# Signs of float64 weights by a ScalarE activation, softmax inverses on GpSimd, and weight scales from whole norms, with a new order

## The chip, the cores and the metric

One core of a Trainium2 chip runs the kernel. A core has a matrix engine (TensorE, PE in the profile; its weight loads are PEld), a vector engine (VectorE, DVE), an activation engine (ScalarE, ACT), GpSimd (POOL) and SyncE (SP), which here only issues DMAs. Each engine works through its own queue in the order in which the program put the instructions there. The metric is the device time of one execution in microseconds (us).

## The reference

Three blocks follow one another: attention with a banded or a strided causal mask, a dense layer with a softmax-weighted activation and a layer norm, and a bilinear layer. All inputs come as float32 here but the weights, which come as float64.

```
def _attn_ref(q, k, v):                       # 4 batches, 8 heads, 576 positions, 64 wide
    scores = scale * np.matmul(q, k.transpose(0, 1, 3, 2))
    ...                                       # heads 0-3: last 32 positions; 4-7: every 32nd
    attn = np.exp(scores - np.max(scores, axis=-1, keepdims=True))
    attn = attn / (np.sum(attn, axis=-1, keepdims=True) + 1e-09)
    return np.matmul(attn, v)

def _moe_ref(x, w_in, w_out, g_ln):           # 2304 tokens, 512 -> 1024 -> 512
    h = x @ w_in
    e = np.exp(h - h_max)
    solu = h * (e / (np.sum(e, axis=-1, keepdims=True) + 1e-09))
    ln = (solu - mu) / np.sqrt(var + 1e-06) * g_ln
    return ln @ w_out

def _moe2_ref(x, w_a, w_b, w_out):            # 512 -> 1536 -> 512
    return (x @ w_a) * (x @ w_b) @ w_out
```

## The kernel before

The kernel collects its work as a list of operations, each with an engine, an estimated duration, the tokens that it reads and writes, and a key. A planner (class `Plan`) orders them: `forward` lists the operations by a model of the engines, taking the ready one with the smallest key; `backward` lists them from the end and gives new keys; `schedule` repeats this `passes` times with some random noise on the keys and keeps the order with the smallest modelled length. The program is then emitted in that order, so every engine's queue is a result of the planner.

The work has these parts:

- *Attention* (`att_tile`): 40 tiles, ten for each of four batches: four strided ones with 6 cells of 54 columns, and six banded ones with 4 or 2 cells of 96. Scores on PE (L700, L703), row maxima on DVE (L716), differences on DVE (L725), exponentials on ScalarE (L728), row sums on DVE (L729), then the inverse of the sums: ScalarE adds a small number and scales (L733), DVE takes the reciprocal (L734). GpSimd multiplies (L767 in batch 0, which goes to PE for its transposes, L763; L778 in the others, which are split into two float16 parts by L785 and L786 and transposed by DMA). The product with V is L797 in batch 0 and L802 to L804 in the others.
- *Weights from float64* (`from_f64`): a DMA brings 128x512 numbers as pairs of 32-bit words into one of three buffers `raw64`. ScalarE scales the upper words, read as float32, by 2^-112 (L462), which moves the exponent; DVE shifts the lower words (L464), merges both (L469), and sets the sign from the upper word (L475), the last reader of the buffer. There are 52 such conversions: 8 for `w_in`, 8 for the first layer's `w_out`, 36 for the bilinear layer's three matrices (12 of them during attention, `early`).
- *First layer* (`moe1`, `s2`): 18 token tiles. The first product h (L855) needs `w_in` in two parts; softmax and layer norm follow (L860 to L884), a DMA transposes, and the second product y (L904) needs all eight pieces of the first layer's `w_out`, split into two float16 parts by ScalarE (L540) and DVE (L542) after a scale that depends on all of them.
- *Bilinear layer* (`product`, `ab`, `out_tile`): products M (L1288) and output products o (L1353), by three passes over parts of the weights. For the scale of a pair of weight tiles the kernel squares both (`norms_ab`, L915, to bfloat16), lets PE sum the squares of each column over the partitions with a matrix of ones (L920, eight matmuls for a pair, collected in the bank `y` or `Q`), and takes the largest (`scale_ab`, from L927).

PSUM bank `y` has one buffer. It is shared by y, the transposes of batch 0 and the norms of the early weights.

## Time and profile before

| what | value |
|---|---|
| median of 3 runs | 745.37 us (742.57 to 747.46) |
| profiled execution | 743.58 us |
| its span | 741.8 us, 14239 instructions |
| PE busy | 713.4 us (96%) |
| DVE busy | 522.9 us (70%) |
| ScalarE busy | 430.1 us (58%) |
| GpSimd busy | 121.8 us (16%) |
| mean granted clock of PE | 0.986 of full speed |

The span runs from the first to the last instruction of the profiled execution; its own time is 1.8 us longer. The page gives, for groups of equal instructions, busy time and mean duration, and beside these the idle time ahead of them with what ended it. DVE and ScalarE instructions overlap their neighbours in the records by some hundredth parts of a microsecond, so sums of durations lie above busy times. Matmuls are pipelined; what one of them costs PE is read from the distance to the next start.

### The profile page before, as it was taken

How to read it: one execution, taken by the hardware profiler on the slowest of the kernel's cores; microseconds unless marked ns; L12 is line 12 of the kernel's file. 1: busy time of each engine (PE TensorE's matmuls, PEld its weight loads, DVE VectorE, ACT ScalarE, POOL GpSimd, SP SyncE). 2: the span in 40 equal slices, each digit the busy share in tenths (PEclk: the TensorE clock that was granted, in tenths of full speed). 3: DMA queues.
4: the chain of work that ended last, by engine and by line, in shares of the span. 5: the costliest groups of instructions: out<-in, count | busy, mean ns of one | idle time of the engine just before them, and what ended most of it. 6: DMA issues, size and time to landing. Idle time of an engine off the chain costs nothing.

```text
span 741.8 us, 14239 instructions
## 1 busy us (share of the span) xinstructions
PE 713.4 (96%) x5516; PEld 474.5 (64%) x5516; DVE 522.9 (70%) x1020; ACT 430.1 (58%) x800; POOL 121.8 (16%) x194
## 2 busy tenths in 40 slices
PE   6889899999999999989999999999999999999997
PEld 4667678878778887867655555555555545555553
DVE  5899989666758676898998998758576454434252
ACT  4678887677678667885767656555272323132230
POOL 5441425243425332120000000000000000000000
PEclk9979899999999999999999999999999999999999
DMA  9889969978683944967547133507505041611304
GB/s 213 198 213 207 212 167 183 228 172 179 123 146 84 232 87 115 272 129 250 198 152 263 33 122 100 163 29 236 197 29 170 1 130 47 230 57 55 117 5 166
DMA packets 159328, 109.62 MB, mean 148 GB/s; under 512 B 103702, under 2 KB 137500, under 8 KB 159260
## 3 DMA queue, kind: packets, MB, share of 16 engines
q1 hardware_dynamic: 159260, 108.71, 56.5%
q8 instruction: 43, 0.70, 0.4%
q14 instruction: 25, 0.20, 0.1%
HBM read 65.42 MB, written 27.53 MB: 125 GB/s over the span
## 4 chain that ended last, share of the span: by engine, by line
PE 89%; DVE 4%; ACT 3%; issue 2%; DMA 1%; POOL 0%; DVEq 0%; ACTq 0%; SPq 0%
PE M L1288 33%; PE o L1353 19%; PE h L855 13%; PE y L904 12%; PE s L703 4%; PE s L618 2%; PE xbank L802 2%; PE xbank L797 1%; ACT qkT L626 1%; PE s L700 1%; DVE wk L863 1%; PE xbank L804 1%; PE xbank L803 1%; DMA raw<-in_moe_w_out_dram 1%; DVE e L725 1%
## 5 line engine op out<-in xcount | busy, mean ns | idle before, releaser
L1288 PE MATMUL M<-y,w 128*128 128x384 f16 x1512 | 256.0, 326 | 0.0
L1288 PEld LDWEIGHTS <-w 128*128 128x128 f16 x1512 | 147.3, 98 | 100.0
L1353 PE MATMUL o<-wo,p 128*128 128x512 f16 x648 | 147.0, 379 | 0.0
L1353 PEld LDWEIGHTS <-p 128*128 128x128 f16 x648 | 63.3, 98 | 71.7
L904 PE MATMUL y<-lnT,wout 128*128 128x256 f16 x864 | 101.1, 273 | 2.4 <-DMA lnT<-ln 1.0
L904 PEld LDWEIGHTS <-wout 128*128 128x128 f16 x864 | 82.1, 98 | 15.4 <-issue 4.8
L855 PE MATMUL h<-win,xh 128*128 128x512 f32 x288 | 79.7, 416 | 4.6 <-DVE wk L863 2.5
L1295 ACT COPY M<-M 128x384 f32<-128x384 f32 x72 | 33.6, 467 | 58.5 <-PE M L1288 58.2
L855 PEld LDWEIGHTS h<-win,xh 128*128 128x128 f32 x288 | 54.2, 196 | 16.3 <-ACT xh L844 3.1
L1360 DVE SCALAR_TENSOR_TENSOR ob<-o,osc,op 128x512 f32<-128x512 f32 x36 | 27.0, 751 | 46.3 <-PE o L1353 41.8
L1338 ACT ACTIVATE p<-A 128x384 f16<-128x384 f32 x72 | 37.2, 522 | 36.0 <-DVE A L1337 35.7
L1299 DVE TENSOR_TENSOR A<-M,V 128x384 f32<-128x384 f32 x36 | 19.9, 555 | 34.7 <-PE M L1288 34.5
L1340 DVE SCALAR_TENSOR_TENSOR p<-A,p 128x384 f16<-128x384 f32 x72 | 39.0, 553 | 7.4 <-ACT p L1338 6.4
L1310 ACT COPY V<-M 128x384 f32<-128x384 f32 x36 | 17.1, 474 | 42.4 <-PE M L1288 42.2
L855 PE MATMUL h<-win,xl 128*128 128x512 f32 x144 | 41.3, 411 | 0.0
L703 PE MATMUL s<-qkT 64*54 64x54 f32 (+2 forms) x672 | 37.2, 247 | 3.3 <-ACT qkT L626 2.3
L462 ACT ACTIVATE f64f<-raw 128x512 f32<-128x512 f32 x52 | 34.8, 672 | 9.1 <-DVE w L1127 4.9
L469 DVE SCALAR_TENSOR_TENSOR f64f<-f64f,raw 128x512 int32<-128x512 int32 x52 | 37.1, 717 | 1.0 <-ACT f64f L462 0.3
L703 PEld LDWEIGHTS s<-qkT 64*54 64x54 f32 (+2 forms) x672 | 26.9, 138 | 14.0 <-issue 3.9
L786 POOL TENSOR_TENSOR P<-e,P 128x324 f16<-128x324 f32 (+2 forms) x30 | 30.7, 1029 | 19.9 <-ACT P L785 19.9
L1337 DVE TENSOR_TENSOR A<-A,M 128x384 f32<-128x384 f32 x36 | 19.9, 553 | 19.5 <-PE M L1288 19.4
L855 PEld LDWEIGHTS h<-win,xl 128*128 128x128 f32 x144 | 28.0, 199 | 6.1
(168 smaller groups left out, 1127.0 us busy)
## 6 DMA issues: line engine op xcount, KB each, us to landing
raw<-in_moe_w_out_dram SPq DMA_DIRECT2D x20, 512.0 KB
o_scr<-ob SPq DMA_DIRECT2D x36, 256.0 KB
op<-o_scr SPq DMA_DIRECT2D x36, 256.0 KB
raw<-in_moe_w_a_dram SPq DMA_DIRECT2D x12, 512.0 KB
raw<-in_moe_w_b_dram SPq DMA_DIRECT2D x12, 512.0 KB
y_scr<-y SPq DMA_DIRECT2D x14, 384.0 KB
y<-y_scr SPq DMA_DIRECT2D x14, 384.0 KB
y_scr<-ys SPq DMA_DIRECT2D x18, 256.0 KB
```

The lines of the kernel that those rows point to most:

```text
L462: act(0.67, lambda: nc.scalar.activation(f(), raw()[:, :, 1].bitcast(F32), AF.Copy, scale=2.0 ** -112), (raw,), (f,))
L469: nc.vector.scalar_tensor_tensor(fi, fi, 3, raw()[:, :, 0], op0=ALU.logical_shift_left, op1=ALU.bitwise_or)
L703: nc.tensor.matmul(s[64 * half:64 * half + nq, f, col:col + kk], g.T()[w, 0, q0:q0 + nq], g.T()[w, 1, k0:k0 + kk], start=False, stop=n == ...
L786: pool(0.15 + 1.4 * pl, lambda: nc.gpsimd.tensor_tensor(plo, ev(), ph, op=ALU.subtract), (e, ("P2", pi, 0)), (("P2", pi, 1),))
L855: nc.tensor.matmul(h()[:, 512 * n:512 * n + 512], xs[xa]()[:, kk], win[wa][:, kk, 512 * n:512 * n + 512], start=(pi == 0 and kk == 0), sto ...
L904: nc.tensor.matmul(y()[:, 256 * mi:256 * mi + 256], wout[:, kk, wa, 128 * m:128 * m + 128], lnT()[:, xa, kk], start=(pi == 0 and kk == 0), ...
L1288: nc.tensor.matmul(bank()[:, :HB], w()[:, wa, a, kk], y7[b]()[:, xa, kk], start=first and pi == 0 and kk == 0, stop=pi == 2 and kk == 1, s ...
L1295: act(TA, lambda: nc.scalar.copy(dst()[:, :HB], src()[:, :HB]), (src,), (dst,))
L1338: act(TA, lambda x=x, v=v: nc.scalar.activation(v(0), x(), AF.Copy, scale=2.0 ** -PEXP), (x,), ((pu, 0, c, t),))
L1340: dve(TD, lambda x=x, v=v: nc.vector.scalar_tensor_tensor(v(1), x(), 2.0 ** -PEXP, v(0), op0=ALU.mult, op1=ALU.subtract), (x, (pu, 0, c, t ...
L1353: nc.tensor.matmul(o(), pus[u]()[:, xa, c, 128 * tt:128 * tt + 128], wo()[:, 2 * u + c, wa], start=(u == 0 and c == 0 and pi == 0), stop=( ...
L1360: dve(0.75, lambda: nc.vector.scalar_tensor_tensor(ob(), o(), osc()[:, tt:tt + 1], op(), op0=ALU.mult, op1=ALU.add), (o, osc, op), (ob,))
```

## The change

- *Signs.* In `from_f64` ScalarE's `Copy` becomes `Prelu` with the same scale and a slope of 2^32 for negative values. A negative number then carries 2^32 more in its exponent field, and the merge's shift by three bits turns that into the sign bit. DVE's sign instruction goes; the merge (now L475) writes the destination and is the buffer's last reader.
- *Inverses.* In `att_tile` the ScalarE addition and DVE's reciprocal become two GpSimd instructions: an addition and a product with constants, and a power with exponent -1 from a small tile of -1.
- *Norms.* `norms_ab` lets ScalarE sum the squares along a row as it squares; `scale_ab` sums these over the partitions with one float32 matmul of two columns (ones 128x128 as weights) and takes the larger of two numbers. The scale is from the norm of a whole half tile, not of its largest column. The PSUM bank is taken only for that product.
- *Planner.* 120 passes instead of 40, a third of the noise, and from the 40th pass on a return to the best keys every 12 passes. Options that weren't in use are removed.

```diff
-PARAM = dict(early=(0,), seed=1, noise=0.3, ... passes=40, e=3,
+PARAM = dict(back=12, first=40, early=(0,), seed=1, noise=0.1, ... passes=120, e=3,
@@ schedule
         for n in range(PARAM["passes"]):
+            if n % PARAM["back"] == 0 and n >= PARAM["first"]:
+                for o, key in zip(self.ops, keys):
+                    o.key = key
+                self.shift = shift
+                self.forward()
             self.backward()
@@ constants
+        nc.gpsimd.memset(mone, -1.0)
@@ from_f64
-            act(0.67, lambda: nc.scalar.activation(f(), raw()[:, :, 1].bitcast(F32), AF.Copy, scale=2.0 ** -112),
-                (raw,), (f,))
+        act(0.67, lambda: nc.scalar.activation(f(), raw()[:, :, 1].bitcast(F32), AF.Prelu, scale=2.0 ** -112,
+                                               alpha=2.0 ** 32), (raw,), (f,))
         dve(0.5, lambda: nc.vector.tensor_scalar(raw()[:, :, 0], raw()[:, :, 0], 29, None,
                                                   op0=ALU.logical_shift_right), (), (raw,))
-        def sign():
-            nc.vector.scalar_tensor_tensor(g().bitcast(I32), raw()[:, :, 1], -2 ** 31, f().bitcast(I32),
-                                           op0=ALU.bitwise_and, op1=ALU.bitwise_or)
-        dve(0.76, merge, (raw,), (f,))
...
-            dve(0.75, sign, (raw, f, *need), w)
+        def merge():
+            nc.vector.scalar_tensor_tensor(g().bitcast(I32), f().bitcast(I32), 3, raw()[:, :, 0],
+                                           op0=ALU.logical_shift_left, op1=ALU.bitwise_or)
+        dve(0.76, merge, (raw, f, *need) if dtok else (raw, *need), w)
@@ att_tile
-        act(0.2, lambda: nc.scalar.activation(s4()[:, :ng], s4()[:, :ng], AF.Copy, scale=u, bias=1e-9 * u), (), ss)
-        dve(0.17, lambda: nc.vector.reciprocal(r()[:, :ng], s4()[:, :ng]), ss, (r,))
+        def inverse():
+            nc.gpsimd.tensor_scalar(s4()[:, :ng], s4()[:, :ng], 1e-9, u, op0=ALU.add, op1=ALU.mult)
+            nc.gpsimd.tensor_tensor(r()[:, :ng], s4()[:, :ng], mone[:, :ng], op=ALU.pow)
+        pool(0.75, inverse, ("small",), (*ss, r))
@@ norms_ab, scale_ab
-        act(0.61, lambda: nc.scalar.activation(sq(), f(), AF.Square), (f,), (sq,))
-            for c in range(4):
-                nc.tensor.matmul(tp()[:, w], onesb, sq()[:, 128 * c:128 * c + 128], start=c == 0, stop=c == 3)
-        pe(4 * 0.06, norms, (sq, "small"), ((tp, i),), 512)
+        act(0.82, lambda: nc.scalar.activation(sq(), f(), AF.Square, accum_out=fro[:, u, m, i:i + 1]), (f,),
+            (sq, ("fro", u, m, i)))
+        pe(0.12, lambda: nc.tensor.matmul(tp()[:, :2], ones_sq, fro[:, u, m], start=True, stop=True),
+           [("fro", u, m, i) for i in range(2)] + ["small"], (tp,), 8)
-            nc.vector.tensor_reduce(x, tp()[:, :256], axis=AX.X, op=ALU.max)
+            nc.vector.tensor_reduce(x, tp()[:, :2], axis=AX.X, op=ALU.max)
```

The planner moves instructions on every engine. Three places follow, each as the program of before and of the change puts it into one queue.

On DVE, the second and third conversion of the first layer's `w_out`, before: shift (L464), merge (L469) and sign (L475), with reciprocals of attention sums (`sm` to `r`) between them.

```order
L464 TENSOR_SCALAR raw_637<-raw_637 128x512
L469 SCALAR_TENSOR_TENSOR f64f<-f64f,raw_637 128x512
L475 SCALAR_TENSOR_TENSOR wout<-raw_637,f64f 128x512
L464 TENSOR_SCALAR raw_678<-raw_678 128x512
L734 RECIPROCAL r<-sm_702 128x2
L469 SCALAR_TENSOR_TENSOR f64f<-f64f,raw_678 128x512
L734 RECIPROCAL r<-sm_727 128x2
L475 SCALAR_TENSOR_TENSOR wout<-raw_678,f64f 128x512
```

The same place on DVE now, where L469 is the shift, L475 the merge, L723 a row sum, and L857 the first row maximum of h:

```order
L469 TENSOR_SCALAR raw_639<-raw_639 128x512
L723 TENSOR_REDUCE sm_727<-e 128x2
L475 SCALAR_TENSOR_TENSOR wout<-f64f,raw_639 128x512
L469 TENSOR_SCALAR raw_669<-raw_669 128x512
L475 SCALAR_TENSOR_TENSOR wout<-f64f,raw_669 128x512
L469 TENSOR_SCALAR raw_702<-raw_702 128x512
L475 SCALAR_TENSOR_TENSOR wout<-f64f,raw_702 128x512
L857 TENSOR_REDUCE st<-h 128x1
```

Three instructions became two and the reciprocals are gone, so eight rows hold three conversions where they held two. Four conversions of `w_out` stand ahead of h's first row maximum in both programs. Up to the last split of `w_out` (L542, row 172 of DVE's queue before; L536, row 132 now) there were 17 signs, 18 shifts, 18 merges and 15 reciprocals; now there are 16 shifts and 16 merges, and the other groups differ by one small reduction each.

On GpSimd, the first products of batch 0, before (L767 the product with the inverse, L491 a split of `w_in`):

```order
L767 TENSOR_TENSOR lnT<-e,r 128x6x54
L491 TENSOR_TENSOR win_108<-f64f,win_107 128x512
L767 TENSOR_TENSOR lnT<-e,r 128x6x54
L491 TENSOR_TENSOR win_108<-f64f,win_107 128x512
L767 TENSOR_TENSOR lnT<-e,r 128x6x54 x2
```

The same place on GpSimd now, where L729 adds and scales, L730 is the power, L764 the product and L485 the split:

```order
L729 TENSOR_SCALAR sm_257<-sm_257 128x6
L730 TENSOR_TENSOR r<-sm_257,small 128x6
L764 TENSOR_TENSOR lnT<-e,r 128x6x54
L729 TENSOR_SCALAR sm_287<-sm_287 128x6
L730 TENSOR_TENSOR r<-sm_287,small 128x6
L764 TENSOR_TENSOR lnT<-e,r 128x6x54
L485 TENSOR_TENSOR win_108<-f64f,win_107 128x512
```

Two instructions stand ahead of each product, and the first split of `w_in` comes behind two products instead of one.

On SP, the first loads before (L568 and L574 are q and k, L585 is v, L457 a float64 load):

```order
L568 DMA rawq<-in_q_dram 96x6x128
L568 DMA rawk<-in_k_dram 96x6x128
L568 DMA rawq<-in_q_dram 96x6x128
L568 DMA rawk<-in_k_dram 96x6x128
L457 DMA raw_177<-in_moe_w_in_dram 128x1024
L585 DMA raws_110<-in_v_dram 18x5x128
```

And now (L562 and L568 are q and k, L579 is v, L465 a float64 load):

```order
L562 DMA rawk<-in_k_dram 96x6x128
L579 DMA raws_110<-in_v_dram 18x6x128 x2
L568 DMA rawq<-in_q_dram 96x6x64
L579 DMA raws_110<-in_v_dram 18x5x128 x2
L568 DMA rawq<-in_q_dram 96x6x64
L568 DMA rawk<-in_k_dram 96x6x64 x2
L465 DMA raw_245<-in_moe_w_in_dram 128x1024
```

The first piece of `w_in` moved behind eight loads of q, k and v; the four loads of strided q and k still come first.

## Rows read from the trace of the kernel before

**Rows 1.** Page, busy time, share of the span, instructions of each engine

```profile
PE 713.4 (96%) x5516; PEld 474.5 (64%) x5516; DVE 522.9 (70%) x1020; ACT 430.1 (58%) x800; POOL 121.8 (16%) x194
```

**Rows 2.** Busy time by stretch, all engines; the columns stand in the first line

```profile
core 0: us, PE busy (x) PEld busy (x) DVE busy (x) ACT busy (x) POOL busy (x), PEclk, DMA share, GB/s
0.00:20.00 20.00, 13.27 (x105) 9.71 (x105) 10.22 (x25) 8.81 (x13) 9.85 (x29) 1.00 1.02 211
20.00:116.00 96.00, 84.06 (x899) 65.95 (x898) 87.65 (x166) 77.10 (x151) 36.04 (x45) 0.89 0.86 195
116.00:280.00 164.00, 163.63 (x1789) 132.81 (x1789) 112.25 (x215) 114.84 (x207) 62.83 (x95) 1.00 0.78 161
280.00:340.00 60.00, 55.02 (x439) 44.94 (x438) 51.73 (x92) 48.34 (x82) 13.06 (x25) 1.00 0.69 184
340.00:741.80 401.80, 397.43 (x2290) 221.11 (x2287) 261.02 (x526) 181.03 (x350) 0.00 (x0) 1.00 0.38 122
```

**Rows 3.** Chain that ended last, 0 to 125 us: start, us, what

```profile
33.92 1.42 DVE raw L464
...
64.48 4.31 DMA raw<-in_moe_w_out_dram
```

**Rows 4.** Waits of PE, 20 to 120 us: total us, times, longest

```profile
PE xbank L797 <- ACT PT L775: 3.5, 1, 3.5
```

**Rows 5.** Line L904, 110 to 125 us: ns min/median/max, first and last start

```profile
L904 PE MATMUL y<-lnT,wout x85: 269/273/283, 109.7 to 121.9; 128*128 128x256 f16 x85
```

**Rows 6.** DVE in order of time: start, us, instruction

```profile
63.74 0.68 DVE L475 SCALAR_TENSOR_TENSOR wout<-raw,f64f 128x512 int32<-128x512 int32 x1
64.34 0.42 DVE L464 TENSOR_SCALAR raw<-raw 128x512 int32<-128x512 int32 x1
...
72.67 0.69 DVE L475 SCALAR_TENSOR_TENSOR wout<-raw,f64f 128x512 int32<-128x512 int32 x1
...
108.73 0.74 DVE L542 SCALAR_TENSOR_TENSOR wout<-wout,gs_sb 128x512 f16<-128x512 f32 x1
```

**Rows 7.** Groups by line: busy us, mean ns, idle before them and releasers

```profile
L475 DVE SCALAR_TENSOR_TENSOR f64f<-raw,f64f 128x512 int32<-128x512 int32 x36 | 25.8, 721 | 0.2
L464 DVE TENSOR_SCALAR raw<-raw 128x512 int32<-128x512 int32 x52 | 27.2, 528 | 4.2 <-DMA raw<-in_moe_w_a_dram 4.2
L462 ACT ACTIVATE f64f<-raw 128x512 f32<-128x512 f32 x52 | 34.8, 672 | 9.1 <-DVE w L1127 4.9 <-DMA raw<-in_moe_w_in_dram 1.8 <-DMA raw<-in_moe_w_a_dram 1.4
L733 ACT ACTIVATE sm<-sm 128x6 f32<-128x6 f32 (+2 forms) x40 | 8.1, 202 | 3.7 <-DVE sm L729 3.6
L734 DVE RECIPROCAL r<-sm 128x6 f32<-128x6 f32 (+2 forms) x40 | 6.7, 171 | 11.3 <-ACT sm L733 11.3
L881 POOL TENSOR_TENSOR st<-st,small 128x1 f32<-128x1 f32 x18 | 11.6, 643 | 1.5
L875 POOL TENSOR_TENSOR st<-st 128x1 f32<-128x1 f32 x18 | 4.8, 269 | 1.5
L874 POOL TENSOR_SCALAR st<-st 128x1 f32<-128x1 f32 x18 | 5.1, 282 | 58.1 <-ACT wk L861 58.0
```

**Rows 8.** PE in order of time, two stretches: start, us, instruction

```profile
100.64 0.21 PE L802 MATMUL xbank<-PT,V 54*64 54x54 f16 x1
...
101.99 1.19 PE L855 MATMUL h<-win,xl 128*128 128x512 f32 x4
...
354.71 0.38 PE L531 MATMUL Q<-2row,ones 1*128 1x2 f32 x2
355.02 3.10 PE L1288 MATMUL M<-y,w 128*128 128x384 f16 x18
...
357.95 0.61 PE L920 MATMUL Q<-sq,onesb 128*128 128x128 bf16 x8
358.40 2.11 PE L1288 MATMUL M<-y,w 128*128 128x384 f16 x12
```

**Rows 9.** GpSimd in order of time: start, us, instruction

```profile
33.34 3.12 POOL L491 TENSOR_TENSOR win<-f64f,win 128x512 fp32r<-128x512 f32 x2
```

More of the change, by code (lines that the diff above doesn't have):

```diff
@@ L52 @@
 PASSES = ((0, 0), (0, 1), (1, 0))
-PARAM = dict(early=(0,), seed=1, noise=0.3, direct=(0,), span=4.0, dense=1500, cols=5000, pf1=(),
-             pf2=(), ph1=(), pv=(), pp=(8,), ps1=(), ps2=(), passes=40, e=3,
+PARAM = dict(back=12, first=40, early=(0,), seed=1, noise=0.1, direct=(0,), span=4.0, dense=1500, cols=5000, ph1=(), pv=(), pp=(8,),
+             passes=120, e=3,
              PT=3, raw=2, rawl=2, raws=2, qkT=2, V=2, wk=2, xt=1, ln=2, lnT=2, ys=2, raw64=3, f64f=4, att=100.0,
@@ L361, in tile_banded_attention_solu_bilinear @@
     wsc = const.tile([128, 2], F32, name="wsc")
-    small = const.tile([128, 48], F32, name="small")
+    small = const.tile([128, 78], F32, name="small")
     wab = small[:, :24].rearrange("p (u i m) -> p u i m", u=NU, i=2)
@@ L932, in scale @@
             nc.vector.reciprocal(x, y)
-        dve(1.03, scale, [(tp, i) for i in range(2)], (("wab", u, m),))
+        dve(0.75, scale, (tp,), (("wab", u, m),))
     def w_src(m, j):
@@ L947, in early @@
         u, i = divmod(j, 2)
[L948 to L951 removed]
+        norms_ab(u, m, i, f)
         if i:
[L953 removed]
+            scale_ab(u, m, rings["y"].new())
     order = [groups[b][pr] for b in range(B) for pr in (2, 3, 0, 1)]
```

36 lines of the change are left out of this document (9 added, 27 removed).

## The prediction

> **What bounds the kernel now.** First I read the busy shares [rows 1]: TensorE (PE) is busy for 713.4 of 741.8 us. Only 28.4 us of its time is idle, and that is nearly all that a better order of work can win. Next I read the same engines by stretch [rows 2]. From 116 to 280 us PE idles 0.4 us, and from 340 us to the end 4.4 us, so relief of other engines is worth nothing there unless PE itself gets less to do. The idle time lies at the start: 6.7 us before 20 us and 11.9 us from 20 to 116 us; another 5.0 us lies from 280 to 340 us. In the second of these stretches VectorE (DVE) is busy for 87.7 of 96 us, more than any other engine.
>
> Then I read the chain that ended last [rows 3]: from 30 us it runs through DVE's shifts and merges of weights, and PE's longest wait between 20 and 120 us, 3.5 us [rows 4], is for a ScalarE copy whose tile is late on DVE. PE pays for such gaps twice: its mean granted clock over 20 to 116 us is 0.89 of the full 2.4 GHz, and 1.00 from 116 us on [rows 2]. If time went with the clock, 84.1 x 0.11 = 9 us of its busy time there would be slowness.
>
> What ends this stage can be named. The first matmul of the second MoE product (y, L904) starts at 109.7 us [rows 5]; DVE's last split of w_out (L542), which it needs, runs from 108.73 to 109.47 us [rows 6]. Soon behind it PE is full. So the question is how much sooner DVE reaches that split.
>
> **The change, part by part.** *Signs.* Each of 52 conversions from float64 loses its third DVE instruction (L475), 0.72 us in the mean [rows 7]. The 24 behind 340 us lie under a full PE and bring nothing. Ahead of the last split of w_out stand 17. DVE instructions overlap their neighbours, so the slot matters too: a sign that starts at 63.74 us is followed at 64.34 us [rows 6], 0.60 us. So 17 x 0.60 to 0.72 = 10.2 to 12.3 us. On ScalarE a Prelu takes the place of a Copy. No Prelu is in the trace; the nearest row is that Copy (L462), 0.67 us [rows 7], and I leave it there. If it took 0.1 us more, the 16 conversions of w_in and w_out would cost ScalarE 1.6 us in a stretch where it idles 18.9 of 96 us. A table switch doesn't arise: in the order of the changed kernel ScalarE has one table load, as before.
>
> *Inverses.* For each attention tile ScalarE's 0.20 us (L733) and DVE's 0.17 us (L734) go; with 15 tiles ahead of the split DVE gets at most 15 x 0.17 = 2.6 us, at least 1.5 us with overlap. GpSimd gets two instructions instead. The first is like L874, 0.28 us. The second is a power on 128 x 2 to 6; the trace has a power on 128x1 alone, L881 with 0.64 us, against 0.27 us for a product of that size (L875) [rows 7]. Lower bound: further columns are free, 0.92 us a tile. Upper bound: the 0.37 us come again for each column, 0.27 + 6 x 0.37 = 2.5 us, 2.8 us a tile. I take 1.0 us, next to the one row of a power. That is 0.6 us more than the two instructions removed, but two hand-overs between busy queues go too: DVE's reciprocals waited 11.3 us in all for ScalarE [rows 7], 0.3 us a tile. So a tile's probabilities come 0.3 us later. PE feels that in the ten tiles of batch 0, whose chain is short of cover; of 3 us I charge a quarter, 0.7 us. Behind the pair GpSimd holds only the product that needs it and later splits; it is busy for 36.0 of 96 us [rows 2], so 15 us more fit.
>
> *Order.* Two conversions that stood ahead of the last split now stand behind it: 2 x (0.53 + 0.72) = 2.5 us without their signs, 2.0 us with overlap. About 1 us of small reductions goes along. In all DVE has 14.5 to 18.4 us less ahead of that split; were DVE the only limit, y would start at 91 to 95 us. Loading stops it earlier. The last piece of w_out was issued at 64.48 us, right as the sign of 63.74 us freed its buffer [rows 6], and landed at 68.8 us [rows 3]. The DMA share from 20 to 116 us is 0.86 [rows 2], so the same bytes at share 1.0 land at 20 + 48.8 x 0.86 = 62 us. From the last sign of w_out (ending 73.4 us) to the last split DVE needed 36 us [rows 6]; without reciprocals and with a little less between, 33. With 4 us for the conversion: 62 + 4 + 33 = 99 us. The first load of w_in also stands behind more of q, k and v now, so DVE has less to fill its early gaps with. I take y's start at 99.7 us, 10 us sooner. PE has one tile's 36 PV matmuls fewer ahead of it and does them later, 1.4 us (100.64 to 101.99 us [rows 8]). The gain is 8.6 us.
>
> *Norms.* Twelve groups of eight 128-column matmuls go from PE, which is full where most of them lie. One group takes 0.45 us of it (357.95 to 358.40 us [rows 8]): 5.4 us. In their place come 12 float32 products with two columns. The nearest are the two records of L531, 0.31 us to the next matmul [rows 8], though with one row of weights instead of 128: 3.7 us. Net 1.7 us won; bounds 5.4 won (free) and 0.7 lost (0.51 us each, the pair's 0.38 us plus a third). ScalarE's square gains an accumulator read, of which I know only that its small instructions take 0.2 us (L733); two thirds of 24 lie under a full PE.
>
> *280 to 340 us.* Of 5.0 us idle [rows 2] the few signs and the lighter DVE queue may give back a part; I take 1.0 us, bounds 0 and 3.
>
> **Sum.** The profiled execution took 743.6 us (span 741.8 us, 1.8 us around it). 743.6 - 8.6 - 1.7 - 1.0 + 0.7 = 733.0 us. It lies 1.8 us below the median of the runs, 745.4 us; carried over, 734.8, so **735 us**.
>
> **The rivals.** *A, loading holds the start back (741 us).* DVE is freed, but the last w_out lands no sooner than 68.8 us. Then y starts at 68.8 + 4 + 33 = 106 us, 3.7 us sooner; less 1.4 us of PV, with 1.7 us of norms, 4 us in all. For it speaks the DMA share, 1.02 in the first 20 us and 0.86 behind it [rows 2]; against it that this load was waiting for a buffer, not for the queue.
>
> *B, the power costs by the column (757 us and more, slower).* At 2.8 us for six columns, 2.1 for four and 1.3 for two, 40 tiles (16, 16, 8) cost GpSimd 88 us, and probabilities come some 2 us later than now. If half of that shows in the ten tiles of batch 0 (10 us) and a fifth in the other thirty (12 us), it gives 757 us. It turns the sign from about 1.8 us a tile on, where half the delay eats the 10 us. For it: 0.37 us over a plain product is much for one column. Against: nothing in the rows says that it comes again with each. The Trainium skill ("GPSIMD Engine Reference", section "When to use GPSIMD") sends elementwise work to VectorE, as about twice as fast; by that factor the pair would cost 0.75 us, but already the rows of one column show 0.92 us.
>
> *C, GpSimd slows DVE (741 us).* A shift (L464) takes 0.53 us in the mean [rows 7], but 1.42 us of the chain went to one at 33.92 us [rows 3], while GpSimd ran a split of w_in from 33.34 to 36.46 us [rows 9]. If each of 15 early pairs held DVE for 0.4 us, 6 us of the gain would go. Against: that split has 512 columns, the pair six.
>
> *D, the new order opens gaps where PE was full (742 to 756 us).* From 116 to 280 us PE has 0.4 us idle, so a product that comes late there costs it directly. Ten gaps of 1 us would eat the gain; the rows can't say how the new order stands there.
>
> **Numbers.** Forecast 0.58; A 0.18, C 0.06, B 0.07, D 0.11. About 1% is what a measurement of this kernel can tell from no change, so faster means below 738 us and slower above 753 us. Nine tenths of the forecast's own range, 726 to 739 us, lie below 738, 0.52; of A, C and D 0.10 do, where norms or the last stage bring more. Faster 0.62. Slower: B and 0.04 of D, 0.11. Same: 0.27. The range reaches down to 725 us (DVE's bound, 5 us, and the norms' bound, 3.7 us, in good part) and up to 746 us, past A, C and half of D; what is left out is B, the rest of D and a little below.
>
> **What would show it.** Right: the second product starts near 100 us, the mean clock over 20 to 110 us is above 0.95, GpSimd's power takes under 0.8 us, and PE idles under 1.5 us from there to 280 us. Wrong: the power's mean above 1.3 us (B); DVE's shifts waiting for loads and the second product at 105 us or later (A); shifts beside the pair at over 1 us (C); PV products that wait for probabilities between 110 and 290 us (D).

## The result, and the profile after

The changed kernel takes **754.11 us** (median of 4 runs, 751.02 to 757.18) against 745.51 us (742.57 to 747.46) for the kernel before, measured beside it: a ratio of 1.0117, 95% interval 1.0090 to 1.0143. I had forecast 735 us and a range of 725 to 746. The change makes the kernel slower, and I had given that 0.11.

The profiled execution of the changed kernel took 757.18 us, with a span of 755.4 us. The four executions lie at 751.0, 751.2, 757.0 and 757.2 us, so this profile, 13.6 us of span above the one before, shows more than the 8.6 us by which the medians differ. The first line of its page that matters is the one that answers to [rows 1]:

```profile
PE 727.3 (96%) x5444; PEld 483.1 (64%) x5444; DVE 480.2 (64%) x928; ACT 428.2 (57%) x784; POOL 170.4 (23%) x275
```

TensorE idles 755.4 - 727.3 = 28.1 us, as much as before (28.4). VectorE lost 42.7 us of work. But TensorE is busy 13.9 us *longer*, with 72 matmul records fewer: the same matmuls take longer. The view by stretch, which answers to [rows 2], says where (same columns):

```profile
0.00:20.00 20.00, 12.91 (x104) 9.54 (x104) 9.02 (x20) 8.12 (x10) 11.84 (x34) 1.00 0.90 181
20.00:116.00 96.00, 87.35 (x834) 68.37 (x834) 68.91 (x128) 70.96 (x131) 58.09 (x76) 0.89 0.79 190
116.00:280.00 164.00, 161.28 (x1753) 129.06 (x1751) 105.16 (x189) 117.82 (x204) 83.09 (x132) 0.96 0.81 177
280.00:340.00 60.00, 57.60 (x427) 47.09 (x426) 43.32 (x79) 42.68 (x67) 16.21 (x34) 0.98 0.51 128
340.00:755.40 415.40, 408.16 (x2334) 229.08 (x2331) 253.84 (x516) 188.61 (x373) 1.19 (x2) 0.99 0.37 123
```

From 20 to 116 us TensorE gets through 834 matmuls where it got through 899, but these are other mixes of narrow and wide ones; by its idle time, 8.7 us for 11.9 at the same clock of 0.89, this stretch is no worse than before. From 116 to 280 us, where it had idled 0.4 us at a granted clock of 1.00, it idles 2.7 us at 0.96. With 0.98 and 0.99 in the last two rows, where before had 1.00, that makes 0.04 x 161 + 0.02 x 58 + 0.01 x 408 = some 12 us of slowness, if time goes with the clock (an estimate), which is most of the 13.9. The second product's matmuls alone are busy for 109.8 us in sum, before for 101.1. By 363 us the difference is there: the last matmul of the second product starts at 363.0 us, before at 346.6, and the bilinear work behind it only starts later. VectorE, which I took for the bound of the second stretch, is now busy for 68.9 of its 96 us; yet the first matmul of that product, the row that answers to [rows 5], starts at 109.1 us and not at my 99.7. (In the kernel before, that line over its whole run first starts at 108.5 us; the 109.7 of [rows 5] was the first in its stretch.)

```profile
L901 PE MATMUL y<-lnT,wout x864: 269/273/421, 109.1 to 363.0; 128*128 128x256 f16 x173
```

**One gap.** TensorE's longest new wait is 5.26 us, at 87 to 93 us. The kernel before has a smaller gap there too: TensorE is busy for 2.14 of the 5 us from 85 us, at a clock of 0.50 behind it. The timelines of GpSimd, ScalarE, VectorE and TensorE there read as a chain (start, us, instruction; in brackets the idle time before it and who ended it). In this kernel L729 and L730 are the pair, L775 is the product with the inverse, L876 and L878 are the layer norm's scale, and L865 is the sum of squares that it waits for:

```profile
81.23 1.33 POOL L730 TENSOR_TENSOR r<-sm,small 128x6 f32<-128x6 f32 x1
82.53 1.87 POOL L775 TENSOR_TENSOR e<-e,r 128x324 f32<-128x324 f32 x2
84.48 0.20 POOL L729 TENSOR_SCALAR sm<-sm 128x6 f32<-128x6 f32 x1
84.76 1.32 POOL L730 TENSOR_TENSOR r<-sm,small 128x6 f32<-128x6 f32 x1
86.19 1.60 POOL L876 TENSOR_SCALAR st<-st 128x1 f32<-128x1 f32 x1
87.88 0.55 POOL L878 TENSOR_TENSOR st<-st,small 128x1 f32<-128x1 f32 x1
...
81.56 0.20 ACT L865 ACTIVATION_READ_ACCUMULATOR ln<-wk 128x1 f32 x1
...
88.46 1.15 ACT L880 ACTIVATE ln<-wk,st 128x1024 f16<-128x1024 f32 x1 [2.41 <-POOL st L878]
...
90.61 0.21 ACT L821 ACTIVATE xT<-xbank 128x64 f32<-128x64 f32 x1
...
90.85 0.15 DVE L516 TENSOR_REDUCE m<-xbank 1x1 f32<-1x2 f32 x1 [3.20 <-ACT xT L821]
...
91.39 1.20 DVE L860 SCALAR_TENSOR_TENSOR wk<-h,wk 128x1024 f32<-128x1024 f32 x1
...
80.98 2.11 PE L852 MATMUL h<-win,xh 128*128 128x512 f32 x8
...
92.66 3.78 PE L852 MATMUL h<-win,xh 128*128 128x512 f32 x8 [5.26 <-DVE wk L860]
```

The scale's input is there at 81.76 us, and GpSimd takes it up at 86.19: 4.43 us in the queue behind a power, two products, and another pair. It then runs for 1.60 us, where it takes 0.27 at other places (see the last section). ScalarE's next instruction waits 2.41 us for it; VectorE waits for a ScalarE copy that stands behind; TensorE waits for VectorE. Over the 18 token tiles of both kernels (start of the scale less end of the accumulator read) this delay was 0.21 us in the mean before and is 1.07 us now. By itself it doesn't set the time: in h2, the fastest kernel below, it is 0.91 us.

The last two lines show the second price. Eight matmuls that took 2.11 us at 81 us take 3.78 us behind the gap. The granted clock says the same in steps of 5 us:

```profile
90.00:95.00 5.00, 2.34 (x6) 1.86 (x7) 4.08 (x10) 4.96 (x11) 1.94 (x5) 0.50 0.82 175
95.00:100.00 5.00, 5.00 (x20) 3.72 (x19) 3.57 (x7) 2.87 (x6) 1.41 (x3) 0.62 1.15 235
100.00:105.00 5.00, 5.00 (x83) 3.56 (x81) 4.58 (x8) 4.08 (x7) 3.62 (x4) 1.00 0.41 110
105.00:110.00 5.00, 5.00 (x105) 3.98 (x105) 3.82 (x10) 3.87 (x8) 2.03 (x3) 0.91 0.56 136
110.00:115.00 5.00, 5.00 (x51) 3.45 (x49) 1.61 (x3) 2.06 (x4) 3.26 (x6) 0.50 0.49 136
```

At 0.50 TensorE is at its lower level, 1.2 GHz. So the gap of 5 us is paid a second time behind it, and that time is booked as busy. The second fall, at 110 us, is not behind a gap: TensorE is busy without a break from 95 us on, and what runs ahead of the fall are 188 matmuls in 10 us, most of them narrow products with V. The run e2 below has the same TensorE queue to the instruction and stays at full clock there, from 95 to 125 us:

```profile
110.00:115.00 5.00, 5.00 (x69) 4.09 (x68) 5.00 (x8) 4.25 (x8) 2.34 (x2) 1.00 0.72 132
```

Why the clock falls in one execution and not in the other, no run shows. Either way the lost clock is booked as busy, so the idle time can stay at 28 us while the span grows by 13.6.

**The wait from 116 to 280 us.** TensorE's one wait in this stretch is 2.72 us, at 217 us, behind a chain of the same kind:

```profile
206.03 2.70 POOL L729 TENSOR_SCALAR sm<-sm 128x2 f32<-128x2 f32 x1
...
211.99 0.35 ACT L782 CAST P<-e 128x192 f16<-128x192 f32 x1 [3.65 <-POOL e L775]
...
217.17 0.23 PE L799 MATMUL xbank<-PT,V 96*64 96x64 f16 x2 [2.72 <-DVE m L516]
```

The pair's first instruction takes 2.70 us here, where its median is 0.21 us. Its power, a split, a second pair and a product follow on GpSimd; ScalarE's cast waits for the product, VectorE for ScalarE (4.37 us at 214.64 us), and TensorE for VectorE.

### The profile page after: what moved, and what is told of

Its sections match the earlier page's. It is cut to its first block, busy times and chain, and to the rows that moved or that the text cites. A ratio compares the mean times of both kernels' runs of the same rounds, so it can differ in the third digit from the quotient of the medians.

```text
span 755.4 us, 14051 instructions
## 1 busy us (share of the span) xinstructions
PE 727.3 (96%) x5444; PEld 483.1 (64%) x5444; DVE 480.2 (64%) x928; ACT 428.2 (57%) x784; POOL 170.4 (23%) x275
## 4 chain that ended last, share of the span: by engine, by line
PE 88%; DVE 4%; POOL 4%; ACT 2%; issue 1%; DMA 1%; POOLq 0%; SPq 0%; DVEq 0%; ACTq 0%
PE M L1279 31%; PE o L1344 18%; PE h L852 13%; PE y L901 12%; PE s L697 4%; PE s L612 2%; PE xbank L799 2%; PE xbank L794 1%; POOL r L730 1%; PE s L694 1%; DVE y L1226 1%; DVE wk L860 1%; PE xbank L801 1%; PE xbank L800 1%; DMA rawk<-in_k_dram 1%
## 5 line engine op out<-in xcount | busy, mean ns | idle before, releaser
L1279 PEld LDWEIGHTS <-w 128*128 128x128 f16 x1512 | 147.9, 98 | 101.1 <-issue 0.7
L901 PE MATMUL y<-lnT,wout 128*128 128x256 f16 x864 | 109.8, 286 | 4.5 <-ACT y L1224 2.6
L901 PEld LDWEIGHTS <-wout 128*128 128x128 f16 x864 | 85.7, 102 | 22.2 <-issue 4.9
L852 PE MATMUL h<-win,xh 128*128 128x512 f32 x288 | 83.2, 431 | 6.1 <-DVE wk L860 6.1
L852 PEld LDWEIGHTS h<-win,xh 128*128 128x128 f32 x288 | 56.0, 204 | 17.8 <-DVE wk L860 6.4
L730 POOL TENSOR_TENSOR r<-sm,small 128x6 f32<-128x6 f32 (+2 forms) x40 | 45.6, 1140 | 3.3
L710 DVE TENSOR_REDUCE mx<-s 128x6 f32<-128x324 f32 (+2 forms) x40 | 19.4, 488 | 28.9 <-PE s L697 28.7
L1328 DVE TENSOR_TENSOR A<-A,M 128x384 f32<-128x384 f32 x36 | 19.9, 552 | 24.1 <-PE M L1279 23.9
```

The costliest lines, as they stand in the source:

```text
L730: nc.gpsimd.tensor_tensor(r()[:, :ng], s4()[:, :ng], mone[:, :ng], op=ALU.pow)
L852: nc.tensor.matmul(h()[:, 512 * n:512 * n + 512], xs[xa]()[:, kk], win[wa][:, kk, 512 * n:512 * n + 512], start=(pi == 0 and kk == 0), sto ...
L901: nc.tensor.matmul(y()[:, 256 * mi:256 * mi + 256], wout[:, kk, wa, 128 * m:128 * m + 128], lnT()[:, xa, kk], start=(pi == 0 and kk == 0), ...
L1279: nc.tensor.matmul(bank()[:, :HB], w()[:, wa, a, kk], y7[b]()[:, xa, kk], start=first and pi == 0 and kk == 0, stop=pi == 2 and kk == 1, s ...
```

## The experiments

I had three theories for the first runs: the power costs more than planned (1), the planner's new order is itself worse (2), GpSimd's small instructions are held up while VectorE runs two-input instructions (3). Kernels of one group ran beside the kernel before (744.8 to 746.0 us in all groups); ratios are to it. The last column adds up ScalarE's waits for GpSimd in each profiled execution. It shows where the pair is felt, but doesn't rank the kernels: e4 and g1 have some of the smallest waits and the longest times.

| kernel | us | ratio, 95% interval | ScalarE waits for GpSimd, us |
|---|---|---|---|
| before | 745.5 | 1 | 15.0 |
| changed | 754.1 | 1.0117, 1.0090 to 1.0143 | 27.4 |
| *order of the changed kernel* | | | |
| e1 product for power | 750.3 | 1.0057, 1.0032 to 1.0081 | 15.3 |
| e2 pair on ScalarE and VectorE | 748.1 | 1.0031, 1.0007 to 1.0056 | 11.2 |
| *order of before* | | | |
| f1 inverses alone | 751.9 | 1.0081, 1.0052 to 1.0109 | 34.7 |
| f2 signs alone | 743.9 | 0.9973, 0.9954 to 0.9993 | 11.9 |
| f4 signs and norms | 742.6 | 0.9956, 0.9936 to 0.9975 | 11.4 |
| f5 all three | 749.1 | 1.0044, 1.0024 to 1.0064 | 33.2 |
| *before, planned again* | | | |
| e4 new settings | 754.9 | 1.0133, 1.0101 to 1.0165 | 9.7 |
| g1 new settings, seed 2 | 756.0 | 1.0149, 1.0122 to 1.0175 | 11.3 |
| g2 old settings, seed 2 | 751.0 | 1.0085, 1.0070 to 1.0100 | 17.9 |
| *changed, price of the pair 0.75 us* | | | |
| h1 seed 2 | 746.0 | 1.0016, 0.9997 to 1.0036 | 26.9 |
| i2 seed 3 | 743.4 | 0.9973, 0.9952 to 0.9995 | 24.8 |
| g3 old settings | 748.5 | 1.0047, 1.0031 to 1.0064 | 23.9 |
| *changed, measured price* | | | |
| g5 seed 1 | 741.4 | 0.9952, 0.9937 to 0.9967 | 13.0 |
| h2 seed 2 | 733.0 | 0.9855, 0.9799 to 0.9910 | 15.1 |
| i3 seed 3 | 741.7 | 0.9941, 0.9915 to 0.9968 | 16.8 |
| h3 old settings | 748.5 | 1.0036, 1.0019 to 1.0053 | 26.2 |
| *signs and norms only, new settings* | | | |
| e3 seed 1 | 741.1 | 0.9939, 0.9912 to 0.9966 | 10.7 |
| i1 seed 2 | 745.4 | 0.9994, 0.9972 to 1.0016 | 15.0 |

### The changed kernel's order, with a cheaper inverse

e1 puts a product in the power's place, which leaves out the normalization of the attention. e2 puts the two instructions of before at the pair's place in the program.

```diff
 e1
-            nc.gpsimd.tensor_tensor(r()[:, :ng], s4()[:, :ng], mone[:, :ng], op=ALU.pow)
+            nc.gpsimd.tensor_tensor(r()[:, :ng], s4()[:, :ng], mone[:, :ng], op=ALU.mult)
 e2
-            nc.gpsimd.tensor_scalar(s4()[:, :ng], s4()[:, :ng], 1e-9, u, op0=ALU.add, op1=ALU.mult)
-            nc.gpsimd.tensor_tensor(r()[:, :ng], s4()[:, :ng], mone[:, :ng], op=ALU.pow)
+            nc.scalar.activation(s4()[:, :ng], s4()[:, :ng], AF.Copy, scale=u, bias=1e-9 * u)
+            nc.vector.reciprocal(r()[:, :ng], s4()[:, :ng])
```

> The changed kernel with every engine's queue in the same order, but GpSimd's second instruction for the inverse is a plain product in place of the power (so the probabilities come out scaled wrongly: the normalization of the attention is left out). Theory 1, the power's price: in the changed kernel a power takes 1.39 us on six columns, 1.07 on four and 0.78 on two, some 0.28 us as a product; 40 tiles give GpSimd 34 us back, the layer norm's scale behind it comes on time, and the time falls from 754 to 738 to 743 us. Theory 2, the new order itself is bad: it stays at 750 us or above. Theory 3, any more instructions on GpSimd are held up by VectorE (a GpSimd instruction on 128x2 took 2.70 us beside VectorE's shifts): it falls by half only, to 746 to 749 us.

> The changed kernel with the same planned order, but at each tile's place in it the inverse is issued to ScalarE and VectorE as before the change. GpSimd gets nothing new. Theory 1 (power's price): 738 to 743 us, about as with the plain product. Theory 2 (the new order): 750 us or above. Theory 3 (GpSimd's instructions are held up by VectorE): clearly below the run with the plain product, 735 to 741 us against 746 to 749.

Measured: 750.3 and 748.1 us against 754.1, with L730's mean at 0.30 us in e1. So with every instruction in the same place the GpSimd inverse costs 6.0 us, and 3.8 of these go with the length of the power. The other 2.2 us are within what the two intervals overlap. e1 just meets what I expected under theory 2 (750 us or above), and e2 lies between the ranges of all three. Even with the cheap inverse this order is no better than that of before.

The profiled executions of the changed kernel and e2 (757.18 and 745.65 us, further apart than the medians) can be laid side by side. TensorE falls 3.7 us behind e2 at 84 to 96 us, where the gap is; another 4.5 us at 104 to 112 us, where nothing is waited for and only the clock differs; and 3.4 us at 196 to 230 us, around the wait of 2.72 us. e1 falls behind at 104 to 112 us as well (its clock is 0.50 from 105 to 110 us), so this second part isn't the power's length.

### Signs and norms, planned without the pair

e3 gives the inverses back to ScalarE and VectorE and lets the planner order anew; e4 is the kernel before with the new settings.

```diff
 e3 (to the changed kernel)
-        pool(0.75, inverse, ("small",), (*ss, r))
+        act(0.2, lambda: nc.scalar.activation(s4()[:, :ng], s4()[:, :ng], AF.Copy, scale=u, bias=1e-9 * u), (), ss)
+        dve(0.17, lambda: nc.vector.reciprocal(r()[:, :ng], s4()[:, :ng]), ss, (r,))
 e4 (to the kernel before)
-PARAM = dict(early=(0,), seed=1, noise=0.3, ... passes=40
+PARAM = dict(back=12, first=40, early=(0,), seed=1, noise=0.1, ... passes=120
```

> The changed kernel without the inverses' move, planned anew: signs by ScalarE, norms from whole half tiles, new planner. Theories 1 and 3: the gains that the prediction saw without GpSimd's part remain, 733 to 739 us. Theory 2 (the planner's new settings give bad orders): 746 to 755 us.

> The kernel before with nothing but the planner's new settings (120 passes, a third of the noise, return to the best keys). Theories 1 and 3: within 742 to 747 us, or a few us less. Theory 2: 750 us or above.

Measured: 741.1 and 754.9 us, e3 between the ranges that I had expected, e4 where theory 2 had it. The order that the new settings find for the *unchanged* work loses 9.4 us. That looked like theory 2, and the next groups were made to part it from the pair's price.

### The parts, one by one, in the order of before

These four leave the planner's costs and settings as they were and change only what a step issues, so TensorE's queue is that of before to the instruction (but for the norms' matmuls).

```diff
 f1
-        act(0.2, lambda: nc.scalar.activation(s4()[:, :ng], s4()[:, :ng], AF.Copy, scale=u, bias=1e-9 * u), (), ss)
-        dve(0.17, lambda: nc.vector.reciprocal(r()[:, :ng], s4()[:, :ng]), ss, (r,))
+        act(0.2, lambda: nc.gpsimd.tensor_scalar(s4()[:, :ng], s4()[:, :ng], 1e-9, u, op0=ALU.add, op1=ALU.mult), (), ss)
+        dve(0.17, lambda: nc.gpsimd.tensor_tensor(r()[:, :ng], s4()[:, :ng], mone[:, :ng], op=ALU.pow), ss, (r,))
 f2: Prelu for Copy; the first merge empty, the sign's place takes the merge
 f4: f2, and accumulated squares with one two-column matmul for a pair
 f5: f1 and f4
```

> The kernel before, each engine's order as it stands there, with one part of the change alone: every tile's 1/(sum) is the addition and the power on GpSimd instead of one instruction on ScalarE and one on VectorE. TensorE's order is that of before to the instruction. If the pair on GpSimd costs what it cost inside the changed kernel's order (750.3 with a product for the power and 754.1 with the power, against 748.1 with the pair on the old engines: 2 and 6 us), this comes out 3 to 8 us above before, 749 to 753, and the trace shows ScalarE waiting at line 881's counterpart (the layer norm's scale) for GpSimd's small instructions more than in before. If the pair only hurts inside the new order, where it stands ahead of other things, this is within 1.5 us of before, 744 to 747.

> The kernel before, in its own order, with the signs alone: ScalarE's rebasing is the Prelu that keeps the sign, and the second two-input instruction on VectorE for each weight piece is gone. About 44 instructions of 0.7 us leave VectorE, 17 of them ahead of the last split of w_out. My prediction gave the part 8.6 us, of which it said that a new order was needed to collect it. If TensorE at 20 to 116 us is held by VectorE in this order, as the idle time ahead of its instructions there says, the gain shows without a new order: 737 to 741. If TensorE's order decides, and VectorE's relief only moves waits from VectorE to weights or to ScalarE, it is 743 to 746.

> The kernel before, in its own order, with the signs and the norms: as the run with the signs alone, and the 96 matmuls for the weights' column norms become 12 of two columns on sums that ScalarE's squares leave beside them. By the prediction's term the norms give 1.7 us more than the signs alone. If TensorE's clock decides (dropping matmuls where TensorE is short of work leaves it emptier, not faster), they give nothing, and this is within 1 us of the run with the signs alone. Either way, if the loss of the changed kernel sits in its order and its GpSimd pair, this one lies under before, and at or under the 741.1 of the changed kernel planned without the pair.

> All three parts of the change in the order of the kernel before (the planner's costs and settings as they were; only what each step issues is changed). If the parts add up, its time is that of the run with signs and norms plus what the inverses alone add to before. The distance from here to the changed kernel's 754.1 is then what the new order costs: 9 us by the run of the planner's settings alone (754.9 against 745.4). If the order of before is merely as bad for these parts, this one is 750 or more.

Measured: inverses +6.2 us, signs -1.8, signs and norms -3.1, all +3.4. The parts add up (6.2 - 3.1 = 3.1), and the pair costs in before's order what it costs in the new one. f4 alone is already faster than both kernels. This also splits the 8.6 us of the change: f5 computes what the changed kernel computes, in before's order (and holds the norms' bank as long as before did), so the pair costs 6.2 to 6.5 us (f1, and f5 less f4), signs and norms give back 3.1, and the order costs the remaining 5 (754.1 against f5's 749.1). I had expected 9 us for the order, from e4.

Since the queues are equal, f1 and before can be laid side by side, instruction by instruction. TensorE is 4.0 us behind from 88 us on, stays there to 240 us, then falls 8 us behind and stays there. The second place, f1's timelines (L882 and L884 are the layer norm's scale, L736 and L737 the pair, L781 the product, L788 ScalarE's cast of it, L910 the copy that frees the bank of the second product):

```profile
237.64 2.62 POOL L882 TENSOR_SCALAR st<-st 128x1 f32<-128x1 f32 x1
...
241.26 1.33 POOL L737 TENSOR_TENSOR r<-sm,small 128x6 f32<-128x6 f32 x1
...
243.30 2.30 POOL L737 TENSOR_TENSOR r<-sm,small 128x6 f32<-128x6 f32 x1
245.57 1.41 POOL L781 TENSOR_TENSOR e<-e,r 128x324 f32<-128x324 f32 x2
...
246.33 0.46 ACT L788 CAST P<-e 128x324 f16<-128x324 f32 x1 [4.25 <-POOL e L781]
...
249.00 0.67 ACT L910 ACTIVATE ys<-y,wsc 128x512 f32<-128x512 f32 x1
...
249.73 1.86 PE L907 MATMUL y<-lnT,wout 128*128 128x256 f16 x8 [2.63 <-ACT ys L910]
```

In before this TensorE instruction starts at 242.89 us without any wait. ScalarE's cast waits 4.25 us for the product behind two pairs; the casts and copies behind it in ScalarE's queue, L910 last, wait along. Summed up for the whole of f1, as ScalarE's waits for GpSimd (total us, times, longest):

```profile
ACT P L788 <- POOL e L781: 20.9, 16, 4.2
ACT wk L870 <- POOL st L868: 11.1, 9, 2.3
ACT ln L886 <- POOL st L884: 2.7, 4, 1.0
```

In the kernel before:

```profile
ACT wk L867 <- POOL st L865: 9.6, 8, 2.8
ACT ln L883 <- POOL st L881: 3.3, 5, 1.0
ACT P L785 <- POOL e L778: 2.1, 4, 1.2
```

The wait for the product rose from 2.1 to 20.9 us. ScalarE's idle time is free until something behind the waiting instruction is wanted; at the second place that is L910's copy. The first place, at 80 to 88 us, I have not followed to its end. I had expected that in f1 the layer norm's scale would be late. It isn't: ScalarE's wait for it is 2.7 us for 3.3, and the scale's mean delay is 0.24 us for 0.21.

f2 shows what the signs did. The stretch from 20 to 60 us in the kernel before (columns as in [rows 2]):

```profile
20.00:60.00 40.00, 33.62 (x348) 26.87 (x346) 36.74 (x66) 29.53 (x64) 18.00 (x15) 0.87 0.82 212
```

The same stretch in f2:

```profile
20.00:60.00 40.00, 39.97 (x363) 32.24 (x362) 28.63 (x55) 30.14 (x66) 16.54 (x16) 1.00 0.89 227
```

VectorE has 8.1 us less to do there, and TensorE's clock rises from 0.87 to 1.00. But little of that is left behind 60 us: the last split of `w_out` starts at 106.83 us instead of 108.73. TensorE keeps 1.9 us of that to 288 us. There, behind a wait of 0.70 us that both programs have, eight matmuls of h take 3.19 us where they took 2.06, and 0.2 us are left at the end of these two profiled executions (spans of 741.2 and 741.8 us). The medians differ by 1.8 us.

### The order: settings, seeds, price

g1 and g2 plan the kernel before again; g3 plans the changed kernel with the old settings; g5 tells the planner the measured price.

```diff
 g1 (to e4), g2 (to before)
-seed=1
+seed=2
 g3 (to the changed kernel): noise=0.3, passes=40, no return
 g5 (to the changed kernel)
-        pool(0.75, inverse, ("small",), (*ss, r))
+        pool(0.75 + 0.155 * ng, inverse, ("small",), (*ss, r))
```

> The kernel before, no part of the computation changed, planned with the new settings (noise 0.1, 120 passes, the return to the best keys every 12) but with another seed. The new settings with their own seed gave 754.9 against 745.4. Theory A, a bad draw: any re-drawn order of these operations may come out some us on either side of another, and before's is a well-chosen draw; then this one comes out elsewhere than 754.9, above 745 and by as much as the draw is bad. Theory B, the settings themselves spoil the order (less noise, less spread): this one is again 752 to 757.

> The kernel before with nothing changed but the seed of its planner, 2 for 1, under the old settings. Theory A, before's order is a lucky draw: this one is slower than before by about what the new settings lose, 749 to 755. Theory B, the new settings are the loss: this one is within 2 us of before, 743 to 748, as the old settings find a good order whatever the seed.

> The changed kernel with all its parts, planned anew with the old settings (noise 0.3, 40 passes, no return). In before's order these parts took 749.1, in their own new order 754.1. If the new settings are to blame, this is at 749 or less. If any new draw is on average worse than before's chosen order, it is 750 to 757.

> The changed kernel with its new settings, but its planner counts the pair on GpSimd at 0.75 us plus 0.155 us for each column (1.68 us for six, as the trace after shows) where it counted 0.75 for any. What is computed does not change, only the order. If the loss after the pair comes from a plan made with the wrong price, so that ScalarE's cast and what is behind it stand where the inverse cannot be ready, this wins back most of it: 744 to 749. If the length of GpSimd's chain itself is the loss (each tile's sum to product is 1.3 us longer wherever it stands), or the draw decides, this is 750 to 757.

Measured: 756.0, 751.0, 748.5, 741.4 us. Two things follow. Three new plans of the unchanged work, e4 among them, all lose 6 to 11 us, under old or new settings: the order of before is a good draw for that work, not what its settings always give. It is no such draw for the changed work, where f5, in before's order, takes 749.1 us. And one number in a cost, the pair's price, moved the changed kernel from 754.1 to 741.4 us. Theory 2 in its plain form (the settings are bad) fell with g2 and g5, though for the unchanged work the new settings stay the worse ones (754.9 and 756.0 us for 745.5 and 751.0). To part price from draw I took two more pairs that differ in the price alone, then a third seed:

```diff
 h1, i2 (to the changed kernel): seed=2, seed=3
 h2, i3 (to g5): seed=2, seed=3
 h3 (to g3)
-        pool(0.75, inverse, ("small",), (*ss, r))
+        pool(0.75 + 0.155 * ng, inverse, ("small",), (*ss, r))
 i1 (to e3): seed=2
```

> The changed kernel with another seed of its planner and nothing else: the pair on GpSimd still counted at 0.75 us. If the wrong price is the loss, this is as slow as the changed kernel, 750 to 757. If the changed kernel has a bad draw, another draw is better: 740 to 748.

> The changed kernel with the measured price in the planner (0.75 us and 0.155 us for each column) and the same other seed. If the price is the loss, this is near the 741.4 of the first seed, 738 to 745, and at least 6 us under the run with this seed and the price of 0.75. If the draw decides, it may be anywhere from 740 to 757, and above or below that run alike.

> The changed kernel with the old settings of the planner and the measured price; with the price of 0.75 these settings gave 748.5. If the price is the loss there too, this is 740 to 745. If the draw decides, within 4 us of 748.5 on either side, 744 to 753.

> Signs and norms with the new settings and the second seed, the inverses on ScalarE and VectorE as before. With the first seed this kernel took 741.1 where the one with the pair on GpSimd at its measured price took 741.4. If the pair gives nothing when it is planned rightly, this is near that seed's 733.0, within 4 us. If the move to GpSimd is worth what leaves the two engines, or the 733.0 is a good draw, this is 738 or more.

> The changed kernel with a third seed, the pair counted at 0.75 us. By the two seeds measured (754.1 and 746.0) 744 to 757, and over the run with the measured price by 6 us or more if the price is the loss.

> The changed kernel with the third seed and the measured price. By the two seeds measured (741.4 and 733.0) 731 to 744 if the price is the loss. If the draw decides and the two pairs so far agreed by chance, anywhere from 733 to 756, above or below the run with the same seed and the price of 0.75 alike.

Measured, wrong price against measured price: 754.1 to 741.4, 746.0 to 733.0, 743.4 to 741.7, and with the old settings 748.5 to 748.5. The price never costs and brings 0 to 13 us. But a new price also makes a new draw, and draws at one price differ by as much: 743.4 to 754.1 us at the wrong one, 733.0 to 748.5 at the measured one. The intervals of i2 and i3 overlap, and h3 shows no gain. By what I had put down before, h2 spoke for the price, and h1, h3 and the pair of i2 and i3 for the draw. So four pairs don't part the two. Whether the planner took it up can be read from ScalarE's waits for GpSimd: with the new settings they fall from 27.4, 26.9 and 24.8 us to 13.0, 15.1 and 16.8; with the old ones they stay at 24 to 26 us, and so does the time. That the third seed gains 1.7 us while its waits fall by 8 shows the limit of this number: a wait costs only where something behind it is wanted. These waits in the changed kernel (line, total us, times, longest):

```profile
ACT P L782 <- POOL e L775: 13.1, 12, 3.7
ACT ln L880 <- POOL st L878: 9.2, 6, 3.3
ACT wk L864 <- POOL st L862: 5.1, 5, 1.4
```

The same waits in g5, where that for the product (L775) has shrunk most:

```profile
ACT wk L864 <- POOL st L862: 5.4, 5, 2.0
ACT P L782 <- POOL e L775: 4.0, 4, 1.5
ACT ln L880 <- POOL st L878: 3.6, 6, 1.1
```

h2 beats both kernels: 733.0 us (730.95 to 739.84), 0.9855 of before. Its profile (an execution of 739.84 us) shows much of what I had forecast for the change. The second product starts at 102.5 us, 6 us sooner than in the kernel before (first line). But the early start isn't what makes it fast: h1 starts that product at 102.7 us (second line) and takes 746.0 us.

```profile
L901 PE MATMUL y<-lnT,wout x864: 269/273/421, 102.5 to 344.4; 128*128 128x256 f16 x173
L901 PE MATMUL y<-lnT,wout x864: 269/273/417, 102.7 to 348.7; 128*128 128x256 f16 x173
```

By stretch, TensorE in h2 idles 2.7 us for 11.9 from 20 to 116 us, and not at all from 116 to 280, where its clock is 0.96 even so:

```profile
20.00:116.00 96.00, 93.27 (x924) 74.63 (x923) 75.98 (x138) 77.47 (x139) 64.18 (x80) 0.93 0.85 196
116.00:280.00 164.00, 164.00 (x1749) 130.32 (x1747) 107.05 (x191) 119.70 (x211) 95.18 (x143) 0.96 0.84 178
```

Is the pair worth having at its true price? With seed 1 no (741.4 with it, 741.1 without), with seed 2 yes (733.0 against 745.4). Two seeds that differ by 0.3 and 12.4 us don't settle it.

## Why the prediction was wrong

**The power's price, "I take 1.0 us, next to the one row of a power".** This step failed. GpSimd's groups by shape in the changed kernel (busy us, mean ns):

```profile
L730 POOL TENSOR_TENSOR r<-sm,small 128x6 f32<-128x6 f32 x16 | 22.3, 1392 | 1.3
L730 POOL TENSOR_TENSOR r<-sm,small 128x4 f32<-128x4 f32 x16 | 17.1, 1071 | 1.3
L878 POOL TENSOR_TENSOR st<-st,small 128x1 f32<-128x1 f32 x18 | 10.1, 563 | 1.5
...
L730 POOL TENSOR_TENSOR r<-sm,small 128x2 f32<-128x2 f32 x8 | 6.2, 776 | 0.7
```

Each column adds about 0.16 us ((1392 - 776) / 4), and one column has 0.56. With the first instruction (0.29 us) a pair for six columns is 1.68 us. All 40 pairs take 59.2 us, 1.48 us each. My bounds, 0.92 to 2.8 us, held it, but for the point I leaned on the only row there was, which could not show how the price grows with columns. Rival B was the right kind of answer at too steep a slope: its rate of 0.37 us a column is more than double the measured one. The Trainium skill ("GPSIMD Engine Reference", section "When to use GPSIMD") puts GpSimd at about half of VectorE's speed in adds, products and maxima of two inputs. Taken as an estimate for the pair (twice the 0.37 us of the two instructions that it replaces, though one of these ran on ScalarE), that gives 0.75 us. The trace has 1.68 us for six columns, so a power can't be priced by that rule.

**The pair's place, "Behind the pair GpSimd holds only the product that needs it and later splits".** This step was wrong as well: it turned 1 us a tile into 0.7 us in all, where f1 measured 6.2. I looked for who waits for the inverse and found the product. I left out that ScalarE's cast waits for the product with all of ScalarE's queue behind it (20.9 us of waits in f1 for 2.1 before). I also left out that the layer norm's scale stands in GpSimd's queue: in the changed kernel's order it is 4.43 us late at 86 us, though in f1 hardly ever. And I charged only the ten tiles of batch 0. Rival B put the turn of the sign at some 1.8 us a tile; at 1.48 us the pair has cost more than signs and norms bring. In f1 both losses fall on later tiles, at 80 to 88 and at 246 to 254 us of its own time.

**The order, "Soon behind it PE is full" and "I take y's start at 99.7 us".** This is the largest miss. The sum had 8.6 us of gain for signs and order together; the runs have 1.8 us for the signs in before's order and a loss of 5 us for this order, some 12 us off. Two things were wrong in it. First, y's start. Loading was not the limit (rival A): in the changed kernel the last merge of `w_out` ends at 68.92 us, 4.4 us sooner than the last sign did (73.36). But from there to the end of the last split it took another 40.5 us (109.42), where I had counted on 33. VectorE wasn't the only limit of these splits; they alternate with h and the layer norm, and so waited for the chain above. Nor is that split what y's start waits for: in the kernel before y starts at 108.5 us, and the split starts at 108.73. Second, the step from y's start to the time. With the measured price and the new settings y starts at 102.1 to 102.5 us, and g5, h2 and i3 take 733 to 742 us; but h1 starts it at 102.7 and takes 746.0, and h3 at 103.9 and takes 748.5. A start some 6 us sooner is not 6 us of time: in h1 TensorE idles 6.5 us from 20 to 116 us where it idled 11.9 before, but its granted clock there is 0.82 where it was 0.89.

**Rival D, "the new order opens gaps where PE was full", at 0.11.** It happened as described, 2.7 us of idle time and a clock of 0.96 from 116 to 280 us, but my reason for keeping it small was that the rows can't speak of it. The runs say why it should have weighed more: a new order is a draw of its own. Three other plans of the unchanged work took 751.0 to 756.0 us, and four plans of the changed work at one price 743.4 to 754.1.

**Signs and norms.** The instruction count and the prices were right: Prelu takes 0.666 us beside Copy's 0.672, and VectorE loses what I said. In the old order the signs gave 1.8 us. The norms gave 1.3 us (f4 less f2, inside both intervals) for my 1.7. From 280 to 340 us TensorE idles 2.4 us for 5.0, at a clock of 0.98; the 1.0 us that I took there can't be told from the rest.

**What stays open.** Why one draw is 8 us better than another was not traced down to single instructions. Open are also what share of the gain with the measured price is the price and what share the draw, whether the pair gains anything under a good plan, and why the clock falls where TensorE had no gap.

## What to carry to other kernels

When a small operation moves to a slower engine, cost it with the width it has here, and list every instruction that the new queue holds behind it and every queue that waits for those; an engine that works in order passes the delay on to work that has nothing to do with it. Where a planner sets the order, measure the new instruction once, put its price in, and plan again before judging the change (here that gave 13, 13, 2 and 0 us). And judge a re-planned kernel by several plans of it: here plans of the same work at the same price lay up to 11 us apart, more than the change that was to be measured. To see what a part costs, hold the order still, as f1 to f5 do.

## What the runs showed of the hardware

GpSimd's smallest instructions took up to ten times their usual time here. The layer norm's 128x1 `TENSOR_SCALAR` takes 0.27 us at 96.31 us and 1.60 us at 86.19 us in the changed kernel, 2.62 us at 237.64 in f1, and 2.76 us already in the kernel before, where it runs beside a sign, two shifts and two merges on VectorE (the lines show it and the merges):

```profile
233.62 2.76 POOL L879 TENSOR_SCALAR st<-st 128x1 f32<-128x1 f32 x1
...
235.05 1.27 DVE L469 SCALAR_TENSOR_TENSOR f64f<-f64f,raw 128x512 int32<-128x512 int32 x2
```

The GpSimd instruction ends at 236.38 us, VectorE's last at 236.32. That fits the row of the Trainium skill ("GPSIMD Engine Reference", section "Specifications") by which GpSimd shares its interfaces to SBUF with VectorE and contends with it when VectorE reads two inputs there. I had named the opposite direction as rival C. No run separates this cause. The layer norm's 18 instructions are held as much before as now (496 ns in the mean before, 504 now). But the pair's own first instruction is held too: it takes 2.70 us at 206.03 us, beside two shifts and two merges of VectorE, and stands at the head of the chain that ends in TensorE's wait at 217 us. So theory 3 may have a part in the loss, and these runs don't give its size.
